# 128 stationary columns for batch 0's value products, and a small rank for the second dispatch in the planned order

## The chip, the core and the metric

The kernel runs on one core of a Trainium2 chip. The metric is device time in microseconds (us) of one execution, from three executions of the kernel, of which the median counts. Beside them stands one profiled execution, whose trace is read below. The engines are PE (TensorE matmul), PEld (TensorE weight load), DVE (VectorE), ACT (ScalarE), POOL (GpSimd) and SP (the engine that issues most of the DMA transfers here).

## What is computed

Four batches of 576 tokens pass through block-causal attention with 8 heads of 64, then a token-mixing layer with two matrices of 512x1024 and 1024x512 and a gate, and then a mixture of eight experts in which each token goes to one expert, all in float32.

```python
scores = scale * np.matmul(q, k.transpose(0, 1, 3, 2))      # 4 batches, 8 heads, 576 x 64
scores = np.where(block_i >= block_j, scores, -1e9)         # blocks of 64
attn = np.exp(scores - max); attn = attn / (attn.sum() + 1e-9)
x = np.matmul(attn, v)                                      # heads side by side: 4 x 576 x 512
...
xk = mu_k * x + (1.0 - mu_k) * x_prev
xr = mu_r * x + (1.0 - mu_r) * x_prev
k = np.maximum(xk @ w_k, 0.0)
x = 1.0 / (1.0 + np.exp(-(xr @ w_r))) * (k * k @ w_v)
...
# one expert e per token, fresh or that of the token before, by a local gate
h = np.maximum(x[b, s] @ w1[e], 0.0)                        # w1: 512 x 1024
out[b, s] = p[e] * (h @ w2[e])                              # w2: 1024 x 512
```

## The kernel before

**The order.** Almost nothing is issued where it is written. Each operation is recorded in a plan, with its engine, an estimated duration and what it depends on, and at the end a list scheduler (`schedule`, L95) simulates the engines and decides the order in which each engine gets its instructions. `Plan.issue` (L273) then emits them, so that nearly every instruction of the trace bears line L282. The hardware doesn't reorder: each engine runs its list in order and waits where an operand isn't ready. Among the operations that are ready on an engine, the scheduler takes the one with the smallest `prio`, which is a due time worked back from the end of the program. To that it adds a rank: `prio -= 1e5 * o[5]` (L109) lowers the number by 100,000 ns of due time where o[5] is true. Before the change o[5] is a yes or no: no for operations recorded under the ranks "ffn" (the expert slots) and "late" (the second dispatch), yes for all else. Where nothing is ready for PE in the first stage, the scheduler puts in a small filler matmul (L1418, `acc<-ones`, bf16).

**Attention.** A unit is one half (256 query rows) of one head of one batch; a half also has its own short list of key chunks. A unit forms scores `s` on PE, maxima `nm` on DVE, exponentials `ea` or `eb` on ACT, transposes them on PE (`psT<-ident,ea` and `psT<-ident,eb`), copies the transposed tiles on ACT to SBUF, and multiplies them with the values (`values`, L651); ACT copies the result to `x`. In batches 1 to 3 scores and values go in two parts each as fp32r, a high and a low one. Batch 0 is `direct` (L513): its matmuls take plain fp32 operands. Its buffers are lent from later stages (`lend`, L403): `v` is one of two tiles of five chunks of 128 keys by 64 columns (tile v itself and the start of tile x_1), the transposed tiles lie in `d`, `xm` and `x_1`. So a value product of batch 0 shows as `acc<-x,v`, `acc<-d,x`, `av<-d,v` and the like, and its form 128*64 is 128 contraction rows by 64 stationary columns; score products and most of the transposes have the form 128*128, and 32 of the transposes (of the first, half-wide key chunk) 128*64. While batch 0 runs, the mixing weights `wk`, `wr`, `wv` are loaded in pieces and split in two by ACT and POOL, after DVE has unpacked them.

**Mixing.** Groups of 256 tokens follow, woven with the attention of batches 1 to 3. Group 0 forms `d` (the difference of neighbouring tokens, POOL), `xm` (DVE), `xh` (ACT) and then multiplies. Its `d` lies in the tile lent to batch 0.

**Experts.** Routing gives each token an expert and a rank. A first dispatch sorts the tokens known by then, and a second one (`dispatch(False)`, L1028, rank "late") sorts the rest: some 60 small DVE operations and a few matmuls that end in `evi` (the expert of each slot, and whether it is another than before), and `gidx` and `sidx` (the token rows that a slot gathers and scatters). Then 19 slots of 128 tokens run (`slot`, L1324). The first seven need only the first dispatch. A slot has POOL gather its rows (`ea<-y_dram,gidx`, L1266), SP read the expert's number from `evi` into a register (L1287 and L1288), SP issue four loads of 512 KB for w1 and four for w2 (L1295) into the only raw buffers that there are (w1: `eb` twice, `qk`, `x`; w2: `x` three times, `d`). Of each such chunk ACT writes the high part and DVE the low part (a 128x1024 subtraction, `wkl<-x,wkh`, `attr<-eb,attr`, `wvl<-eb,wvh`, `xl<-d,kkl`): I call these the wide splits. A raw buffer is free for the next slot's load once DVE has made the low part. The split weights of even and odd slots lie in two sets of tiles (even: w1 in attr, w2 in wkh and wkl; odd: w1 in wvh and wvl, w2 in kkh, xh, kkl, xl). PE transposes the rows, ACT and DVE split them (`wrl<-psT,wrh`, 128x512), PE multiplies with w1, ACT applies relu, PE transposes again and multiplies with w2, ACT scales the result into `xm`, and POOL scatters it (`out<-xm,sidx`, L1275).

Of the kernel before, what the change touches and what calls it, by code (L numbers as in the profile page):

```python
# [9 lines left out]
F32 = mybir.dt.float32  # L10
# [10 lines left out]
B, H, S, D = 4, 8, 576, 64  # L21
# [163 lines left out]
class Plan:  # L185
# [87 lines left out]
    def issue(self):  # L273
        ops = self.ops
        until = next(i for i, o in enumerate(ops) if o[0] == "pe" and o[3][0].tensor.name == self.bank)
        start, order = schedule([(o[0], o[5], o[6], o[8], o[9], o[7][0] not in ("ffn", "late")) for o in ops], until if self.warm else -1, 54.0)
        for i in order:
            if i < 0:
                self.warm()
                continue  # L280
            o = ops[i]
            o[2](*o[3], **o[4])  # L282
# [3 lines left out]
def fused_kernel(ctx: ExitStack, tc: tile.TileContext, a, out):  # L286
# [3 lines left out]
    pe, act, dve, pool, sp = (Engine(plan, n, e) for n, e in zip(  # L290
        ("pe", "act", "dve", "pool", "sp"), (nc.tensor, nc.scalar, nc.vector, nc.gpsimd, nc.sync)))
# [73 lines left out]
    a1 = att.enter_context(tc.tile_pool(name="a1", bufs=1))  # L365
# [3 lines left out]
    def buffers(where, name, shape=None, dtype=F32, n=1):  # L369
        if name not in rings:  # L370
            rings[name] = [0] + [where.tile(shape, dtype, name=f"{name}_{i}") for i in range(n)]
        return rings[name]

    def ring(*args):

        r = buffers(*args)
        r[0] += 1
        return r[1 + (r[0] - 1) % (len(r) - 1)]

    def flat(x):  # L380
        return x.rearrange("p a b -> p (a b)")
# [19 lines left out]
    lent = {}  # L401

    def lend():  # L403
        x0, x1 = (flat(buffers(m1, f"x{i}", [128, 4, (321, 257)[i]], F32, 2)[2]) for i in range(2))
        th = buffers(m1, "th", [128, DM], F32, 2)[1:]
        relu = buffers(m1, "relu", [128, 512], F32, 2)[1:]
        d = flat(buffers(m1, "d", [128, 4, GT])[1])
        xm = flat(buffers(m1, "xm", [128, 2, GT])[1])
        raw = buffers(a1, "wraw", [128, 512], F32, 2)[1:]
        lent["qk"] = [buffers(a1, "qk", [128, NQ + S], F32, 1)[1], x0[:, 0:NQ + S]]  # L410
        lent["v"] = [flat(buffers(a1, "v", [128, 5, D], F32, 1)[1]), x1[:, 0:320]]
        lent["pt00"], lent["pt01"], lent["pt12"] = [d[:, 0:256]], [d[:, 256:640]], [d[:, 640:1024]]
        lent["pt10"], lent["pt11"] = [xm[:, 0:256]], [x1[:, 320:832]]

        for n in ("qk", "pt00", "pt10"):
            for x in lent[n]:
                dve.memset(x[64:128, :], 0.0)
        lent["w"] = [*relu, *th, *raw]
        lent["wt"] = [xm[:, 256:512]]
        lent["avt"] = [x[:, n:n + 256] for n in (0, 256) for x in raw]  # L420

    def borrow(name):
        if not lent:
            lend()
        lent[name].append(lent[name].pop(0))
        return lent[name][-1]
# [82 lines left out]
    class Unit:  # L509
# [35 lines left out]
        def load_v(self):  # L545
            if self.other:
                self.v = self.other.v
                return
            if self.direct:
                self.v = borrow("v").rearrange("p (c d) -> p c d", d=D)  # L550
            else:
                self.v = ring(a1, "v", [128, 5, D], F32, 1)
            sp.dma_start(self.v[:, 0:self.nv, :], a["v"][self.b, self.h][:, 0:self.nv, :])

        def prep_v(self):
# [95 lines left out]
        def values(self):  # L651
            if self.direct and self.half:
                self.av = av = buffers(psA, "acc", [128, 512], F32, 2)[2]
            else:
                self.av = av = ring(psA, "av", [128, 512], F32, 1)
            for c, (t, o, q) in self.at.items():
                hi, lo = (x[:, o:o + 256 - q] for x in self.pt[t])
                last = c == max(self.at)
                if self.direct:
                    pe.matmul(av[0:64, q:256], self.v[:, c, :], hi, start=(c == 0), stop=last)  # L660
                    continue
                if not last:
                    pe.matmul(av[:, q:256], self.vs[:, c, :], hi, start=(c == 0), stop=False)
                if c:
                    pe.matmul(av[0:64, q:256], self.vs[:, c, 0:D], lo, start=False, stop=False)
                if last:
                    pe.matmul(av[:, q:256], self.vs[:, c, :], hi, start=False, stop=True)
# [21 lines left out]
    class First(Unit):  # L689
# [5 lines left out]
        def load(self):  # L695
            self.q0 = 0
            if not lent:
                lend()
            qk = ring(a1, "qk", [128, NQ + S], F32, 1)
            self.q, self.k = qk[:, 0:NQ], qk[:, NQ:NQ + 512]  # L700
            r = 64 if self.b == 0 else 128
            sp.dma_start(qk[0:r, 0:NQ + 512], a["qk0"][self.b, 0:r])
# [579 lines left out]
    def expert(j, always):  # L1282

        e, i = (evi[0], j) if j < EARLY else (evi[1], j - EARLY)

        def issue():
            regs[j] = (nc.sync.value_load(e[0:1, 0, i:i + 1], min_val=0, max_val=NE - 1),  # L1287
                       None if always else nc.sync.value_load(e[0:1, 1, i:i + 1], min_val=0, max_val=1))  # L1288

        return plan.add("sp", "expert", issue, ins=[e], hold=0.0, late=1250.0)  # L1290

    def load(j, raw, src, at):
        def issue():
            e, new = regs[j]
            nc.sync.dma_start(raw, src(e), **({} if new is None else {"cond": new}))  # L1295

        plan.add("sp", "load", issue, outs=[raw], after=[at], hold=800.0 if j >= SLOTS else 400.0)
# [54 lines left out]
    def tiles(ns, count, out, ins, stationary, moving):  # L1352


        def issue():
            for i in ns:
                for t in range(4):
                    nc.tensor.matmul(out[t * ROWS:t * ROWS + ROWS, :], stationary(i, t), moving(i, t),
                                     start=(i == 0), stop=(i == count - 1))

        plan.add("pe", "tiles", issue, outs=[out], ins=ins + [out] * (ns[0] > 0), hold=1000.0)
# [117 lines left out]
```

## Time and profile before

| quantity | value |
|---|---|
| three executions, median | 798.25 us (796.76 to 800.64) |
| profiled execution | 800.11 us, of which its span 798.4 us |
| PE busy | 770.8 us (97% of the span), 5051 instructions |
| PEld busy | 635.1 us (80%) |
| DVE busy | 605.5 us (76%) |
| ACT busy | 535.6 us (67%) |
| POOL busy | 290.9 us (36%) |

A timeline row gives the start and duration of an instruction, the engine, the line, the operation, its result and operands (buffer numbers left out), shapes, and in brackets how long the engine had been idle before it and what ended that. A row of the windows gives, for a stretch of the span, the busy time of each engine, then the granted clock of TensorE (1.00 is full speed), the share of the DMA engines that were busy, and the rate moved. Busy PE is not PE at its peak: the ends of matmuls are modelled, and a matmul that follows another closely overlaps it in the records.

### The profile page before, as it was taken

How to read it: one execution, taken by the hardware profiler on the slowest of the kernel's cores; microseconds unless marked ns; L12 is line 12 of the kernel's file. 1: busy time of each engine (PE TensorE's matmuls, PEld its weight loads, DVE VectorE, ACT ScalarE, POOL GpSimd, SP SyncE). 2: the span in 40 equal slices, each digit the busy share in tenths (PEclk: the TensorE clock that was granted, in tenths of full speed). 3: DMA queues.
4: the chain of work that ended last, by engine and by line, in shares of the span. 5: the costliest groups of instructions: out<-in, count | busy, mean ns of one | idle time of the engine just before them, and what ended most of it. 6: DMA issues, size and time to landing. Idle time of an engine off the chain costs nothing.

```text
span 798.4 us, 14950 instructions
## 1 busy us (share of the span) xinstructions
PE 770.8 (97%) x5051; PEld 635.1 (80%) x5051; DVE 605.5 (76%) x1301; ACT 535.6 (67%) x1156; POOL 290.9 (36%) x275
## 2 busy tenths in 40 slices
PE   8999999999999999999999998999998999999993
PEld 8665798988989989898997977778876767677872
DVE  6987757876678769587786489899998978588820
ACT  3888567893578946266893525688848968678830
POOL 3334585543745537264452324121121202122100
PEclk9999999999999999999999999999999999999997
DMA  8566311221223202201310005201546377782032
GB/s 218 156 184 192 108 57 55 90 72 36 78 65 101 95 22 83 70 36 37 100 46 27 2 26 194 85 27 41 171 159 247 118 275 250 240 304 97 31 132 64
DMA packets 40466, 87.62 MB, mean 110 GB/s; under 512 B 6540, under 2 KB 10640, under 8 KB 40384
## 3 DMA queue, kind: packets, MB, share of 16 engines
q1 hardware_dynamic: 37152, 76.71, 29.6%
q0 software_dynamic: 3232, 9.90, 3.4%
q8 instruction: 41, 0.67, 0.4%
q14 instruction: 41, 0.34, 0.1%
HBM read 131.68 MB, written 9.90 MB: 177 GB/s over the span
## 4 chain that ended last, share of the span: by engine, by line
PE 67%; issue 12%; DVE 7%; DMA 6%; ACT 5%; POOL 2%; SPq 0%; POOLq 0%; ACTq 0%
PE acc L282 37%; PE s L282 13%; PE psT L282 8%; PE av L282 6%; PE acc L1418 2%; ACT attr L282 2%; DMA out<-xm,sidx 2%; DMA out<-v,ssum 1%; DMA ea<-y_dram,gidx 1%; DVE xm L282 1%; DMA qk<-in_w 1%; ACT ea L282 1%; DMA wraw<-in_w 1%; DVE attr L282 1%; DMA th<-in_w 1%
## 5 line engine op out<-in xcount | busy, mean ns | idle before, releaser
L1275 POOL DMA_INDIRECT out<-xm,sidx x19 | 22.1, 1162 | 174.9 <-ACT xm L282 172.3
L282 DVE TENSOR_REDUCE nm<-s 128x1 f32<-128x576 f32 (+4 forms) x132 | 67.7, 547 | 21.2 <-ACT s L282 20.2
L282 PE MATMUL acc<-xh,wkh 128*128 128x256 f32 x288 | 81.4, 292 | 0.3 <-DVE rk L282 0.3
L282 PE MATMUL acc<-xl,wkh 128*128 128x256 f32 x288 | 81.1, 289 | 0.7 <-POOL xl L282 0.6
L282 PE MATMUL acc<-xh,wkl 128*128 128x256 f32 x288 | 80.5, 288 | 0.0
L282 POOL TENSOR_TENSOR attr<-qk,attr 64x512 fp32r<-64x512 f32 (+1 forms) x48 | 66.9, 1393 | 37.1 <-ACT attr L282 32.4
L282 PE MATMUL av<-attr 128*128 128x256 f32 (+3 forms) x336 | 78.2, 287 | 0.1
L282 DVE TENSOR_TENSOR attr<-psT,attr 64x256 fp32r<-64x256 f32 (+2 forms) x120 | 63.0, 525 | 15.9 <-ACT attr L282 13.6
L282 POOL TENSOR_TENSOR kkl<-relu,kkh 128x512 fp32r<-128x512 f32 x36 | 46.6, 1297 | 56.8 <-ACT kkh L282 47.3
L282 PE MATMUL s<-attr 128*128 128x288 f32 (+3 forms) x288 | 67.1, 299 | 0.0
L282 POOL TENSOR_TENSOR xl<-xm,xh 128x512 fp32r<-128x512 f32 x36 | 46.4, 1288 | 51.9 <-ACT xh L282 46.9
L282 PE MATMUL acc<-attr,wrh 128*128 128x512 f32 x160 | 60.2, 409 | 0.0
L282 ACT ACTIVATE attr<-psT 64x256 fp32r<-64x256 f32 (+2 forms) x120 | 53.4, 462 | 9.2 <-PE psT L282 6.9
L282 PE MATMUL acc<-wvh,kkh 128*128 128x512 f32 x144 | 56.4, 416 | 1.9 <-ACT th L282 1.9
L282 DVE TENSOR_TENSOR wrl<-psT,wrh 128x512 fp32r<-128x512 f32 x57 | 39.2, 687 | 24.2 <-ACT wrh L282 23.8
L282 ACT ACTIVATE xh<-xm 128x512 fp32r<-128x512 f32 x36 | 22.7, 631 | 49.9 <-DVE xm L282 48.8
L282 PE MATMUL acc<-wvh,kkl 128*128 128x512 f32 x144 | 55.6, 413 | 0.0
L282 PE MATMUL acc<-wvl,kkh 128*128 128x512 f32 x144 | 55.2, 408 | 0.0
L282 PEld LDWEIGHTS av<-attr 128*128 128x128 f32 (+1 forms) x336 | 51.5, 166 | 4.7 <-issue 0.6
L282 PEld LDWEIGHTS acc<-xh,wkh 128*128 128x128 f32 x288 | 53.3, 189 | 2.2 <-ACT s L282 0.5
L282 PEld LDWEIGHTS acc<-xl,wkh 128*128 128x128 f32 x288 | 53.4, 189 | 1.9 <-POOL xl L282 1.1
L282 PE MATMUL psT<-ident,eb 128*128 128x128 f32 (+1 forms) x288 | 54.2, 277 | 0.0
(355 smaller groups left out, 2393.1 us busy)
## 6 DMA issues: line engine op xcount, KB each, us to landing
x<-in_w SPq DMA_DIRECT2D x76, 512.0 KB
eb<-in_w SPq DMA_DIRECT2D x38, 512.0 KB
qk<-in_qk SPq DMA_DIRECT2D x24, 544.0 KB
qk<-in_w SPq DMA_DIRECT2D x19, 512.0 KB
d<-in_w SPq DMA_DIRECT2D x19, 512.0 KB
wraw<-in_w SPq DMA_DIRECT2D x24, 256.0 KB
y_dram<-th SPq DMA_DIRECT2D x18, 256.0 KB
v<-in_v SPq DMA_DIRECT2D x28, 160.0 KB
```

The lines of the kernel that those rows point to most:

```text
L282: o[2](*o[3], **o[4])
L1275: plan.add("pool", "scatter", lambda: nc.gpsimd.indirect_dma_start(out=out, out_offset=bass.IndirectOffsetOnAxis(ap=at.bitcast(U32), axis= ...
L1418: plan.warm = lambda: pe.matmul(first[:, 0:128], ones, ones, start=True, stop=True)
```

## The change

In batch 0 a value product takes two neighbouring chunks of `v` as its stationary operand, 128 columns instead of 64. The first 64 columns give the wanted result in rows 0 to 63, and the other 64 give rows 64 to 127, which nobody reads. So that the last chunk has a neighbour, the tiles grow from five to six chunks, the sixth being zeros from two new memsets, and one lent tile moves by 64 columns. The second part replaces the yes or no of the rank by a number: 0 for "ffn", 0.2 for "late", 1 for all else. At L109 that is 20,000 ns of due time by which the second dispatch goes ahead of the expert slots' operations. The changed file is four lines longer from `lend` on, so that L1287 is there L1291, and L1295 is L1299.

```diff
-        start, order = schedule([(o[0], o[5], o[6], o[8], o[9], o[7][0] not in ("ffn", "late")) for o in ops], until if self.warm else -1, 54.0)
+        start, order = schedule([(o[0], o[5], o[6], o[8], o[9], {"ffn": 0.0, "late": 0.2}.get(o[7][0], 1.0)) for o in ops], until if self.warm else -1, 54.0)
...
-        lent["v"] = [flat(buffers(a1, "v", [128, 5, D], F32, 1)[1]), x1[:, 0:320]]
+        lent["v"] = [flat(buffers(a1, "v", [128, 6, D], F32, 1)[1]), x1[:, 0:384]]
+
+        for x in lent["v"]:
+            dve.memset(x[:, 320:384], 0.0)
...
-        lent["pt10"], lent["pt11"] = [xm[:, 0:256]], [x1[:, 320:832]]
+        lent["pt10"], lent["pt11"] = [xm[:, 0:256]], [x1[:, 384:896]]
...
-                self.v = ring(a1, "v", [128, 5, D], F32, 1)
+                self.v = ring(a1, "v", [128, 6, D], F32, 1)[:, 0:5, :]
...
-                    pe.matmul(av[0:64, q:256], self.v[:, c, :], hi, start=(c == 0), stop=last)
+                    pe.matmul(av[:, q:256], self.v[:, c:c + 2, :].rearrange("p c d -> p (c d)"), hi,
+                              start=(c == 0), stop=last)
```

The order on PE hardly changes in batch 0, but the form does. About in the middle of the batch there stands in PE's row before (the last numbers are the stationary columns by the moving ones):

```order
L282 MATMUL psT_140<-ident,eb_147 128x128 x3
L282 MATMUL acc_152<-xm_129,v_133 64x256
L282 MATMUL av_141<-d_128,v_133 64x256 x2
L282 MATMUL s_0_134<-qk_132 128x192
L282 MATMUL acc_152<-x_1_123,v_133 64x256
L282 MATMUL psT_139<-ident,ea_136 64x128
```

and in the changed kernel:

```order
L282 MATMUL psT_140<-ident,eb_147 128x128 x3
L282 MATMUL acc_152<-xm_129,v_133 128x256
L282 MATMUL av_141<-d_128,v_133 128x256 x2
L282 MATMUL acc_152<-x_1_123,v_133 128x256
L282 MATMUL psT_139<-ident,ea_136 64x128
L282 MATMUL s_0_134<-qk_132 128x192
```

The value products have 128 columns now, the one transpose has 64 as before, and a score product moved behind them.

On DVE the second dispatch ends in `gidx_110`. Before, its end stands among the splits of slot 6's w2 (`wkl`):

```order
L282 TENSOR_TENSOR evi_107<-es 1x18
L282 CAST evi_107<-es 1x18
L282 TENSOR_TENSOR wkl<-x_0_122,wkh 128x1024
L282 TENSOR_TENSOR wkl<-x_1_121,wkh 128x1024
L282 COPY d_inv_191<-s_0_134 128x110
L282 TENSOR_TENSOR wrl<-psT_140,wrh 128x512
L282 TENSOR_TENSOR d_inv_191<-d_inv_191 128x22
L282 TENSOR_TENSOR wkl<-x_1_123,wkh 128x1024
L282 TENSOR_SCALAR gidx_110<-d_inv_191 128x18
L282 TENSOR_TENSOR wkl<-d_128,wkh 128x1024
```

In the changed kernel it stands at the start of the splits of slot 4's w2 (`wkl`) and of slot 5's w1 (`wvl`):

```order
L282 COPY d_inv_191<-s_0_134 128x110
L282 TENSOR_TENSOR evi_107<-es 1x18
L282 CAST evi_107<-es 1x18
L282 TENSOR_TENSOR d_inv_191<-d_inv_191 128x22
L282 TENSOR_TENSOR wkl<-x_0_122,wkh 128x1024
L282 TENSOR_SCALAR gidx_110<-d_inv_191 128x18
L282 TENSOR_TENSOR wvl<-eb_147,wvh 128x1024
```

Eighteen wide splits and six of the 128x512 splits, which stood ahead of `gidx_110`, stand behind it now; ahead of `evi_107<-es` there are 16 and 5 fewer. The first operation of this dispatch after the routing, `d_sob`, moved by 11 wide splits.

On SP the reading of `evi_107` (slot 7's expert) stands before behind the last loads of slot 6's w2 (`x_1_123`, `d_128`), and slot 7's first load follows it:

```order
L1295 DMA x_1_123<-in_w 128x2x512
L1295 ISA
L1295 DMA d_128<-in_w 128x2x512
L1287 TENSOR_LOAD evi_107
L1287 ISA x2
```

and in the changed kernel between the last load of slot 5's w2 (`d_128`) and the first load of slot 6's (`x_0_122`):

```order
L1299 DMA d_128<-in_w 128x2x512
L1291 TENSOR_LOAD evi_107
L1291 ISA x2
L1292 TENSOR_LOAD evi_107
L1292 ISA x2
L1299 ISA
L1299 DMA x_0_122<-in_w 128x2x512
```

Slot 7's loads can stand among those of slot 6's w2 there, while before all of slot 6's loads had to be issued first.

## Rows read from the trace of the kernel before

**Rows 1.** Windows of batch 0: busy time of each engine, granted clock, DMA, GB/s

```profile
20.00:40.00 20.00, 20.00 (x106) 13.09 (x103) 18.48 (x43) 16.91 (x58) 7.58 (x10) 1.00 0.53 156
40.00:60.00 20.00, 19.93 (x104) 12.13 (x104) 16.32 (x44) 16.21 (x53) 7.98 (x11) 1.00 0.63 184
60.00:80.00 20.00, 20.00 (x101) 11.49 (x102) 14.86 (x37) 16.90 (x57) 9.28 (x12) 1.00 0.61 190
80.00:92.00 12.00, 12.00 (x107) 8.34 (x106) 8.87 (x24) 8.63 (x21) 6.15 (x8) 1.00 0.37 105
```

**Rows 2.** Chain of waits, 20 to 92 us: its shares, then start, us, link

```profile
by line: PE s L282 28.8%; PE acc L282 26.8%; PE psT L282 24.2%; PE av L282 12.4%; PE acc L1418 4.9%; ACT ea L282 1.4%; ACT x L282 0.7%; ACT wrh L282 0.5%; issue 0.3%; ACT s L282 0.1%; ACTq L282 0.0%
...
23.54 0.57 PE av L282 x2
...
49.71 0.76 PE s L282 x4
...
53.42 0.58 PE acc L282 x2
53.99 0.43 PE av L282 x2
...
54.98 0.33 PE psT L282 x3
...
59.99 0.48 PE psT L282 x3
...
89.15 0.79 PE acc L282 x4
```

**Rows 3.** Timeline of PE, one row of the same stretch

```profile
54.82 0.49 PE L282 MATMUL psT<-ident,ea 128*128 128x128 f32 x3
```

**Rows 4.** Weight loads grouped by form, 20 to 92 us: busy, mean ns, idle

```profile
L282 PEld LDWEIGHTS s<-x 128*128 128x128 f32 x48 | 7.9, 193 | 1.7 <-issue 1.1 <-ACT wkh L282 0.4
...
L282 PEld LDWEIGHTS av<-d,v 128*64 128x64 f32 x24 | 2.9, 136 | 2.0 <-issue 0.7 <-ACT eb L282 0.2
```

**Rows 5.** Timeline of POOL at the end of batch 0

```profile
90.03 1.89 POOL L282 TENSOR_TENSOR d<-x 128x1024 f32<-128x1024 f32 x1 [0.35 <-PE acc L282]
```

**Rows 6.** Windows of the second dispatch

```profile
560.00:580.00 20.00, 20.00 (x99) 16.06 (x98) 19.34 (x54) 16.79 (x22) 2.89 (x3) 1.00 0.53 170
...
600.00:610.00 10.00, 6.76 (x26) 5.19 (x27) 7.21 (x7) 7.64 (x11) 2.63 (x2) 0.83 1.03 395
```

**Rows 7.** Timeline of DVE around the second dispatch

```profile
545.66 0.17 DVE L282 CAST d_sob<-so 128x8 bf16<-128x8 f32 x1
...
552.96 1.22 DVE L282 TENSOR_TENSOR xl<-d,kkl 128x1024 fp32r<-128x1024 f32 x1
...
594.75 0.16 DVE L282 TENSOR_SCALAR gidx<-d_inv 128x18 int32<-128x18 f32 x1
```

**Rows 8.** DVE groups by form, 545.6 to 594.8 us: busy, mean ns, idle

```profile
L282 DVE TENSOR_TENSOR wrl<-psT,wrh 128x512 fp32r<-128x512 f32 x12 | 8.2, 686 | 1.3 <-ACT wrh L282 1.3
L282 DVE TENSOR_TENSOR wkl<-x,wkh 128x1024 fp32r<-128x1024 f32 x6 | 7.2, 1210 | 0.0
```

**Rows 9.** Timeline of POOL: the scatters of slots 3 to 6

```profile
572.44 1.02 POOL L1275 DMA_INDIRECT out<-xm,sidx  x1 [9.51 <-ACT xm L282]
...
585.55 1.49 POOL L1275 DMA_INDIRECT out<-xm,sidx  x1 [12.09 <-ACT xm L282]
...
603.00 1.69 POOL L1275 DMA_INDIRECT out<-xm,sidx  x1 [4.42 <-ACT xm L282]
...
616.90 1.03 POOL L1275 DMA_INDIRECT out<-xm,sidx  x1 [10.70 <-ACT xm L282]
```

**Rows 10.** Timeline of SP, ACT and PE, the stretch of Rows 7

```profile
593.54 0.99 SPq L1295 DMA_DIRECT2D eb<-in_w  x2
...
602.06 0.67 ACT L282 ACTIVATE xm<-s,pslot 128x512 f32<-128x512 f32 x1
...
568.23 0.39 PE L282 MATMUL s<-xl,wrh 128*128 128x512 f32 x1
...
602.78 0.50 PE L282 MATMUL s<-wkh,wrh 128*128 128x512 f32 x1 [2.85 <-ACT xm L282]
```

## The prediction

> **What bounds the kernel now.** The two parts of the change act in two stages, so each is read from its own. The first view is the windows of batch 0 [rows 1]: PE is busy 19.93 to 20.00 of every 20 us at full granted clock from 20 to 92 us, while DVE sums to 58.5 and ACT to 58.6 of the 72 us. The chain of waits of that stretch [rows 2] says the same by another road: its shares of PE are 28.8 + 26.8 + 24.2 + 12.4 + 4.9, 97% in all. The reader is to see that in batch 0 hardly a wait of PE for anyone counts, so that what PE does not have to do is time, up to the point at which DVE or ACT ends last.
>
> The same chain shows that this busy PE loses time. It gives each link the time that PE really moved on. A pair of 256-column value products that follows another pair took 0.43 us (the second link at 53.99), a pair that follows something else 0.58 (at 53.42): entering a run of value products costs 0.15 us. Three transposes took 0.33 us behind a score product (54.98) and 0.48 behind value products (59.99): leaving a run costs 0.15 as well. The score products cost no such thing: four in 0.76 us (at 49.71) [rows 2], 0.19 each for 224 columns, is 0.85 ns a column, and the pair at 53.99 has 0.43 / 512 = 0.84. What the value products have and the scores have not is the form 128*64, the fp32 matmul with 64 stationary columns [rows 4].
>
> The third view is the second dispatch, where the end of the kernel is decided by the slots' scatters [rows 9]. They follow each other in 13.11 us (572.44 to 585.55), then 17.45 (to 603.00) and 13.90 (to 616.90). Two regular spacings would be 26.2 us; 31.35 were taken, so 5.1 us are lost at slot 5 and 6. The rows of the other engines say why [rows 10]: SP issued slot 7's first weight load at 593.54 only, ACT took that slot's high parts in the order written for it, with slot 5's result `xm` (602.06) queued behind them, and PE waited 2.85 us for `xm` (602.78). From 600 to 610 us PE was busy 6.76 of 10 us at a granted clock of 0.83 in the mean [rows 6]: some of that time TensorE ran at 1.2 GHz instead of 2.4, after the wait. SP couldn't issue earlier since slot 7's expert comes out of the second dispatch, whose DVE part ran from 545.66 to 594.75 [rows 7] between the wide splits.
>
> **Part one, the value products.** It adds no matmul and no column that streams: the stationary operand grows, the moving one doesn't. It removes the entry and the exit of each run of value products. I counted 38 runs in batch 0, the first and last of them at 23.54 and 89.15 [rows 2]. 38 x (0.15 + 0.15) = 11.4 us of PE time: by window 9 runs and 2.7 us from 20 to 40, 11 and 3.3 from 40 to 60, 18 and 5.4 from 60 to 92. What it could cost is the longer weight load: 193 ns against 136 in the mean [rows 4], 57 ns more, and 128 such loads' matmuls make 7.3 us if each were exposed and nothing if hidden. I take nothing, because the score products have loads of 128 columns, and by the 0.85 ns a column above they lose no time to them. So PE's own saving lies between 4.1 and 11.4, and I take 11.4.
>
> How much of it becomes time depends on who is late next. DVE has idle time of 1.5, 3.7, 5.1 and 3.1 us in the four windows and ACT 3.1, 3.8, 3.1 and 3.4 [rows 1]. The first window can give at most 1.5, the second 3.3 (PE's own), the last two together 5.4 (PE's own, against 6.5 and 8.2 idle): 10.2 us is the cap. The other end is the one window where both engines have more idle time than PE saves, 3.3 us. After a saving of 10 DVE and ACT would be busy 58.5 of 62 us, and every unit passes from PE to DVE and ACT and back, so some of the room will be waits. I take the middle, 7 us, and keep 3.3 and 10.2 for the range. The time carries on: group 0's `d` on POOL starts 0.35 us after the last value product at 90.03 [rows 5] and the mixing hangs on it.
>
> The rest of part one is small. Two memsets of 128x64 on DVE at the start are of the size of the smallest instructions there, 0.17 us each by `d_sob` [rows 7], and the start of the program waits for loads; 0 to 0.3 us, and I take 0. The lent tile that moves keeps its size and its users.
>
> **Part two, the second dispatch.** Nothing is added; it moves. 18 wide splits and 6 of the 128x512 ones now stand behind `gidx`. A wide split takes 1210 ns alone and a 128x512 split 686 [rows 8], some 0.08 less when they follow closely: 18 x 1.13 + 6 x 0.6 = 24 us by which `gidx` comes earlier, at 571 instead of 594.75. By 16 and 5 of them `evi` comes 21 us earlier. SP then has slot 7's expert long before a raw buffer is free, and its loads start when DVE has freed the buffers of slot 6's w1 instead of at 593.54. The 5.1 us lost at slots 5 and 6 should go: 0 if something else holds slot 7 as late, 5.1 if nothing does.
>
> What is pushed back pays. Of the 49.1 us of the dispatch [rows 7] some 25 wide and 12 short splits take 25 x 1.13 + 12 x 0.6 = 35.5, so 13.6 us are dispatch proper. Splits that stood ahead of it are late by up to that. The split `xl<-d,kkl` (slot 3's last chunk of w2) ended at 554.18 [rows 7] and PE first used it at 568.23 [rows 10]: 14 us of cover, just enough. DVE is busy 19.34 of 20 us there [rows 6], so it catches up only as the dispatch ends, and each raw buffer is freed as much later, with SP's next load queued on it. I take 1.6 us of new waits on PE between 545 and 580, with 0 and 5 as the ends. SP's new wait for `evi`, at about 569, has slot 6's w2 loads queued behind it; these can't start before slot 5's w2 is split, which stands later in DVE's row, so I cost it at nothing; if that cover were gone it is the load of one chunk late. Part two: 5.1 - 1.6 = 3.5 us, between 0 and 5.1 (the lower end below nothing is the last rival).
>
> **The sum.** 7 + 3.5 = 10.5 us. The profiled execution took 800.11 us (1.7 of them outside its span), so it would be 789.6; it lies 1.9 above the median of 798.25, within the runs shown, so the same difference goes to the median: 798.25 - 10.5 = 787.75, put as 787.8.
>
> **Rules beside the rows.** Three transposes stand in one row [rows 3], which carries the form of the first; the second of them has 64 stationary columns. Their link took 0.33 us (at 54.98) [rows 2], the plain 0.11 each, so a transpose of 64 among others of 128 costs nothing there. The Trainium skill, in "TensorEngine Tiling (Array Packing)", Tiling Modes, Key Properties, says that a change of the tiling mode, not of the tile alone, drains TensorE. By that, the losses at the value products' entries and exits would be drains, as the rows agree, but the transposes with 64 columns, which remain, would drain too; there the rows do not agree. "TensorE: Matmul & The Clock Gate", Part 3, The mechanism, of the Trainium skill says that a weight load overlaps running matmuls only where its row group differs. By that the longer loads of full height would be exposed; the score products above speak against it.
>
> **The rivals.** (A) All of PE's saving and all of part two arrive: 10.2 + 5.1 = 15.3, so 783.0. For it: 97% of the chain on PE. Against it: DVE's 18.48 of 20 in the first window. (B) DVE and ACT take PE's place in batch 0: 3.3 + 3.5 = 6.8, so 791.4. For it: 58.5 busy of some 62; against it: the idle time of both is spread, and they have room now. (C) The loss moves to the transposes: with the scores and values at 128 columns the 32 transposes of 64 pay 0.30 us each, 9.6 of the 11.4; 1.8 + 3.5 = 5.3, so 793.0. This is what the drain rule would do; the row at 54.82 speaks against it. (D) The longer loads are exposed: 4.1 + 3.5 = 7.6, so 790.7. (E) The change doesn't do what it says, since the entries and exits come from the alternation of buffers and not from the 64 columns: nothing in batch 0, and 798.25 - 3.5 = 794.8. (F) Slower: the dispatch put first on a DVE with no room starves slots 3, 4 and 5 of their splits, each of which then costs what slot 5 and 6 lose now, 5.1 us: 15.3 lost against 5.1 won and 7 in batch 0, so 801.5, and 805 with 3.3 in batch 0. It decides once PE's waits for splits between 545 and 590 us pass 12.1 us. For it: 19.34 of 20 busy and 14 us of cover against 13.6 of delay. Against it: most splits are late by less, as the dispatch is still spread among 14 or more of them.
>
> **How the numbers follow.** The forecast has 0.48, A 0.16, B 0.13, C 0.04, D 0.04, E 0.08, F 0.07. About 0.5%, 4.0 us, is what a measurement of this kernel can tell from no change; that puts the bounds at 794.3 and 802.2. Below 794.3 lie the forecast, A, B, C and D, 0.85, where what strays out of them makes up for the part of E that comes in with 5.1 from part two. Within lie the rest of E and the nearer half of F, 0.11; above 802.2 the farther half of F, 0.04. The range runs from 781.5 (A with all 11.4 us of PE's saving instead of 10.2 gives 781.75) to 793.5 (just beyond C), and leaves out E and F, 0.15, and a little of A.
>
> **What the profile after would show.** In the chain of batch 0, pairs of 256-column value products at 0.43 us wherever they stand, and three transposes in 0.33 us behind them; the last value product some 7 us before 90.03. If it is B, PE's busy time in the windows falls below 19, with waits for DVE and ACT; if C or D, PE stays at 20 of 20 and the entries or single records stay long. In the second stage, `gidx` about 24 us earlier relative to slot 3's scatter, slot 7's first load not behind slot 6's last, scatters of slots 5 and 6 some 13 us apart, and no stretch with a granted clock of 0.83 there. I am wrong on the whole if PE's waits for splits from 545 to 590 us sum to more than 5, or if batch 0 ends less than 3 us earlier.

## The result, and the profile after

| | before | changed kernel |
|---|---|---|
| median | 798.51 us (796.76 to 802.08) | 791.70 us (787.76 to 794.12) |
| ratio, 95% interval | | 0.990 (0.9874 to 0.9926) |
| profiled execution, of which span | 800.11, 798.4 us | 787.76, 786.0 us |

The change makes the kernel faster by about 8 us by the ratio, 6.8 by the medians. The forecast was 10.5 us, with a range that holds the measured time. The profiled execution of the changed kernel is the fastest of its six, and the one before lay above its median, so the spans differ by 12.4 us where the medians differ by 6.8. A second execution was therefore profiled (e3 below, 791.8 us), and a reading counts here where both traces have it.

The windows of batch 0 in the changed kernel, with columns as in [rows 1]:

```profile
20.00:40.00 20.00, 19.71 (x117) 16.64 (x115) 19.18 (x46) 18.04 (x62) 9.00 (x12) 1.00 0.61 178
40.00:60.00 20.00, 19.00 (x110) 15.60 (x110) 19.26 (x46) 17.66 (x60) 8.80 (x12) 1.00 0.72 206
60.00:80.00 20.00, 19.59 (x131) 15.73 (x130) 19.38 (x45) 18.01 (x57) 9.51 (x14) 1.00 0.53 167
```

PE, first, is no longer busy all of the time (19.00 to 19.71 of 20 us), and DVE, third, is about as full as PE, at 19.18 to 19.38 (18.33 to 19.26 in the second trace) where it had 14.86 to 18.48. Pieces of the chain of waits in the changed kernel (start, us, link), which answer to [rows 2]:

```profile
57.29 1.45 PE s L282 x6
58.74 0.43 PE acc L282 x2
59.17 0.11 PE psT L282
59.28 0.35 PE s L282 x2
59.63 0.33 PE psT L282 x3
59.96 0.43 PE acc L282 x2
```

A pair of value products behind a score product (58.74) or behind transposes (59.96) takes 0.43 us, as only a later pair did before, and the transpose behind it (59.17) takes 0.11: both the entry and the exit are gone. (The six score products of the first piece are four of 224 columns and two of 288.) The end of batch 0, on POOL, answers to [rows 5]:

```profile
82.66 1.90 POOL L282 TENSOR_TENSOR d<-x 128x1024 f32<-128x1024 f32 x1 [0.56 <-PE acc L282]
```

It came 7.37 us earlier. The scatters of slots 3 to 6 answer to [rows 9]:

```profile
564.76 1.87 POOL L1279 DMA_INDIRECT out<-xm,sidx  x1 [9.84 <-DMA x<-in_w]
...
582.74 2.08 POOL L1279 DMA_INDIRECT out<-xm,sidx  x1 [14.78 <-ACT xm L282]
...
597.02 1.02 POOL L1279 DMA_INDIRECT out<-xm,sidx  x1 [10.30 <-DVE wvl L282]
609.25 1.57 POOL L1279 DMA_INDIRECT out<-xm,sidx  x1 [9.03 <-ACT xm L282]
```

The spacings were 13.1, 17.5 and 13.9 us. Now they are 18.0, 14.3 and 12.2: the wait didn't go, it moved one slot forward. Rows of the changed kernel's timeline around it, of DVE, SP, ACT and PE, which answer to [rows 7, 10]:

```profile
560.43 0.16 DVE L282 TENSOR_SCALAR gidx<-d_inv 128x18 int32<-128x18 f32 x1
...
565.13 0.34 SPq L1299 DMA_DIRECT2D eb<-in_w  x1
567.65 0.34 SPq L1299 DMA_DIRECT2D qk<-in_w  x1
...
572.93 1.06 ACT L282 ACTIVATE attr<-qk 128x1024 fp32r<-128x1024 f32 x1 [2.68 <-DMA qk<-in_w]
573.89 0.58 ACT L282 ACTIVATE wrh<-psT 128x512 fp32r<-128x512 f32 x1
...
574.52 0.50 PE L282 MATMUL s<-wkh,wrh 128*128 128x512 f32 x1 [2.18 <-ACT wrh L282]
```

The window of the changed kernel in which the wait lies, with columns as in [rows 6]:

```profile
570.00:580.00 10.00, 7.82 (x29) 5.76 (x28) 7.23 (x7) 5.23 (x7) 0.00 (x0) 0.83 0.91 324
```

`gidx` stands 4.3 us ahead of slot 3's scatter; before, it stood 22.3 behind it [rows 7, 9]. So the second dispatch is 26.6 us earlier on DVE relative to the slots. But ACT now waits 2.68 us for the third chunk of slot 6's w1 (`qk`), slot 4's `wrh` is queued behind that, PE waits 2.18 us for `wrh`, and the mean granted clock of these 10 us falls to the 0.83 that stood at 600 to 610 us before [rows 6]. The second trace has the same 0.83 from 572 to 582 us. PE's waits from 525 to 620 us in the changed kernel (engine, result, line, what it waited for: us in total, times, longest):

```profile
PE s L282 <- ACT wrh L282: 2.2, 1, 2.2
PE psT L282 <- ACT relu L282: 1.8, 1, 1.8
PE acc L282 <- ACT wrh L282: 0.6, 1, 0.6
PE s L282 <- DVE wrl L282: 0.5, 1, 0.5
```

The first and the third are the waits between 545 and 590 us, 2.8 us in all, and 4.0 in the second trace.

### The profile page after: what moved, and what is told of

It is laid out like the page before. It is cut to its first block, busy times and chain, and to the rows that moved or that the text cites. A ratio compares the mean times of both kernels' runs of the same rounds, so it can differ in the third digit from the quotient of the medians.

```text
span 786.0 us, 14915 instructions
## 1 busy us (share of the span) xinstructions
PE 758.1 (96%) x5036; PEld 639.2 (81%) x5036; DVE 608.6 (77%) x1303; ACT 534.7 (68%) x1156; POOL 299.8 (38%) x275
## 4 chain that ended last, share of the span: by engine, by line
PE 57%; issue 13%; DMA 11%; DVE 10%; ACT 7%; POOL 1%; SPq 1%; POOLq 0%; DVEq 0%; ACTq 0%
PE acc L282 34%; PE s L282 10%; PE psT L282 7%; PE av L282 5%; DMA out<-xm,sidx 3%; DMA d<-in_w 2%; DVE xm L282 2%; DMA th<-in_w 2%; DMA out<-v,ssum 1%; ACT attr L282 1%; DVE nm L282 1%; ACT ea L282 1%; DVE attr L282 1%; PE acc L1422 1%; DVE wraw L282 1%
## 5 line engine op out<-in xcount | busy, mean ns | idle before, releaser
L1279 POOL DMA_INDIRECT out<-xm,sidx x19 | 27.9, 1471 | 164.8 <-ACT xm L282 137.1
```

The lines of the kernel that those rows point to most:

```text
L1279: plan.add("pool", "scatter", lambda: nc.gpsimd.indirect_dma_start(out=out, out_offset=bass.IndirectOffsetOnAxis(ap=at.bitcast(U32), axis= ...
```

## The experiments

### The two parts apart

e1, part one alone (of a changed line, only the term that changes is shown, here and in e2 and e7):

```diff
-{"ffn": 0.0, "late": 0.2}.get(o[7][0], 1.0)
+o[7][0] not in ("ffn", "late")
```

> Part one alone: the value products of batch 0 with 128 stationary columns, the second dispatch without a rank of its own, as before. Theory: batch 0 carries all of the gain and the second dispatch none. Group 0's d on POOL starts near 82.7 us as in the changed kernel (90.03 before), slots 4 to 6 are scattered with the spacings of before (one of about 17.5 us, then about 14), and the time is 7 to 9 us below the kernel before, 789.5 to 791.5, as fast as the changed kernel or faster. Rival, the terms of the prediction: part two carries 3.5 us, so this kernel is 7 us below before and 3 to 4 us slower than the changed one.

Measured: 791.98 us, ratio 0.9907 (0.988 to 0.9934). `d` started at 83.07 us; the spacings at slots 4 to 6 were 13.0, 18.1 and 13.1.

e2, part two alone:

```diff
-o[7][0] not in ("ffn", "late")
+{"ffn": 0.0, "late": 0.2}.get(o[7][0], 1.0)
```

> Part two alone: the second dispatch with rank 0.2, the value products with 64 columns as before. Theory: the wait at slot 5 goes, but a new one at slot 4 takes its place (SP reads slot 7's expert and issues more loads into a fuller DMA, ACT waits for slot 6's w1 with slot 4's products queued behind), so the time is within 1.5 us of the kernel before, 797 to 800; in the trace a spacing of some 18 us at slot 4 instead of 17.5 at slot 5. Rival, the term of the prediction: 3.5 us faster than before, 795, with spacings of 13 at slots 4 to 6.

Measured: 800.74 us, ratio 1.0015 (0.9997 to 1.0034); `d` at 89.96, spacings 17.4, 16.0 and 12.2. The two longest of PE's waits from 500 to 620 us there, in the same columns as above:

```profile
PE s L282 <- ACT wrh L282: 3.6, 2, 2.9
PE psT L282 <- ACT th L282: 2.1, 2, 1.6
```

Part one carries all of the result, and part two nothing that can be told from zero. The term of 3.5 us falls.

e3, the changed kernel once more:

> The changed kernel once more, for a second trace and more times. Theory: the wait at slot 4 lies in the order and not in one execution, so the second trace has a spacing of 17 to 19 us there again; the times are 788 to 794 with a median near 791.5. Rival: the wait is an accident of the one execution, the second trace has spacings of 12.5 to 14 at slots 3 to 6, and what differs between executions (787.8 to 794.1) is this wait.

Measured: 792.50 us (790.79 to 795.53), ratio 0.9916 (0.989 to 0.9943), `d` at 83.03, spacing 19.2 us at slot 4, ACT's wait for `qk` 3.6 us. The wait lies in the order; the rival is out.

### What ends batch 0 now

e4 leaves out an operation of the unpacking, and the scheduler plans without it:

```diff
-                    dve.scalar_tensor_tensor(top, low, 29, top, op0=ALU.logical_shift_right, op1=ALU.bitwise_or)
```

> The changed kernel, without the last of the three DVE operations that unpack each half chunk of the mixing weights (the three lowest bits of their mantissas are left out): 48 operations of some 0.5 us less on DVE, nearly all of them in batch 0. Theory: after the change DVE (with ACT fed by it) ends last in batch 0, so with DVE relieved by some 20 us PE is the bound again and group 0's d on POOL starts 3 to 4 us earlier than in the changed kernel, at 78.5 to 80 us instead of 82.66, the whole 3 to 4 us faster than the changed kernel. Rival: the passing from engine to engine or ACT alone sets the end of batch 0, d starts at 82 to 83 and the time stays.

Measured: 793.76 us, ratio 0.991 (0.9872 to 0.9948), `d` at 85.22, later than in the changed kernel, though DVE was busy only 10.78 of the 20 us from 60 to 80. This decides nothing: the scheduler, given other durations, had made another order, and two things were changed at once.

e5 mends that. The plan records the operation in full, and what is issued works on 8 columns, so the order is exactly that of the changed kernel:

```diff
-                    dve.scalar_tensor_tensor(top, low, 29, top, op0=ALU.logical_shift_right, op1=ALU.bitwise_or)
+                    plan.add("dve", "scalar_tensor_tensor", part, (top, low, 29, top),
+                             dict(op0=ALU.logical_shift_right, op1=ALU.bitwise_or))
...
+    def part(o, x, n, y, **kw):
+        nc.vector.scalar_tensor_tensor(o[:, 0:8], x[:, 0:8], n, y[:, 0:8], **kw)
```

> The changed kernel in exactly its own order, but the third of the three DVE operations that unpack each half chunk of the mixing weights works on 8 of its 256 columns (the lowest bits of the rest are left out): some 48 operations of about 0.1 us in place of about 0.5, 18 us less on DVE in batch 0. Theory: DVE ends last in batch 0 after the change, so group 0's d on POOL starts 3 to 4 us earlier, at 78.5 to 80 us in place of 82.66 and 83.03 in the two traces, and the whole is 2 to 4 us faster than the changed kernel. Rival: ACT (18.0 of 20 us busy in a window) or the passing between engines sets the end of batch 0: d starts at 82 to 83.

Measured: 790.75 us, ratio 0.9879 (0.9846 to 0.9912), `d` at 81.00. The window from 20 to 79 us of e5, with columns as in [rows 1]:

```profile
20.00:79.00 59.00, 58.09 (x356) 48.45 (x355) 48.48 (x137) 54.00 (x179) 26.46 (x36) 1.00 0.63 190
```

The same window of the changed kernel:

```profile
20.00:79.00 59.00, 57.30 (x345) 47.07 (x343) 56.82 (x132) 53.45 (x177) 26.64 (x35) 1.00 0.63 187
```

DVE had 8.3 us less to do in this stretch, not the 18 that I expected (32 narrowed operations of 0.19 us fell into it, where I had counted 48 of 0.1, and 5 more of DVE's instructions), and batch 0 ended 1.7 us earlier than in the first trace of the changed kernel, 2.0 than in the second: half of what the theory asked for. So DVE is a part of what ends batch 0 now; relieved of it, ACT has 54.0 of 59 and PE 58.1. The time of the whole, 790.75 us, can't be told from that of the changed kernel. The shares of the chain of waits in the changed kernel from 20 to 92 us answer to [rows 2] (the last 9 us lie behind batch 0, and the view breaks off at its right edge):

```profile
by line: issue 12.1%; PE s L282 9.9%; PE acc L282 9.3%; PE acc L1422 8.3%; DVE nm L282 7.2%; DVE xm L282 7.2%; PE psT L282 6.8%; ACT eb L282 5.5%; ACT ea L282 5.2%; DVE relu L282 4.6%; DVE wraw L282 4.2%; ACT d L282 3.2%; ACT wvh L282 2.5%;
```

PE has about a third of it, where it had 97%, and DVE and ACT most of the rest. In the second trace, from 20 to 84 us, PE has a fifth, and POOL's splits of the mixing weights stand in the chain. So no single engine ends batch 0 now.

e12, part one for the second halves only, without part two:

```diff
+                if self.direct and not self.half:
+                    pe.matmul(av[0:64, q:256], self.v[:, c, :], hi, start=(c == 0), stop=last)
+                    continue
                 if self.direct:
```

> Part one for the second halves of batch 0's heads alone (those with the longer list of keys): their value products have 128 stationary columns, the first halves' 64 as before; the second dispatch as before. In PE's row 17 runs of products with 64 columns are left of 38, so by 0.30 us each PE saves 6.3 us instead of 11.4. Theory: PE's saving becomes time one for one until DVE and ACT end last, so group 0's d on POOL starts 5.5 to 6.3 us before 90.03, at 83.7 to 84.5, not far from the 82.5 to 83.5 of the full change; in what is left of the 64-column runs the first pair still takes 0.58 us. Rival: each run removed is worth the same, about two thirds of its price, all the way: 90.03 less 7.1 x 21 / 38 = 3.9 us, d at 86.1.

Measured: 793.02 us, ratio 0.9943 (0.9926 to 0.9959). The start of `d` in its timeline:

```profile
84.78 1.90 POOL L282 TENSOR_TENSOR d<-x 128x1024 f32<-128x1024 f32 x1 [0.21 <-ACT wvh L282]
```

Two links of its chain of waits, start, us and link:

```profile
49.44 0.43 PE acc L282 x2
49.88 0.58 PE av L282 x2
```

The shares of the chain in e12 from 20 to 84 us:

```profile
by line: PE s L282 32.6%; PE psT L282 21.5%; PE acc L282 20.3%; PE av L282 17.4%; ACT ea L282 1.6%; POOL attr L282 1.6%; DVE xm L282 1.3%; ACT wkh L282 1.0%; issue 1.0%; PE acc L1425 0.9%; DVE attr L282 0.6%; DVE ea L282 0.6%; DVE th L282 0
```

Two pairs, one behind the other: the one with 128 columns takes 0.43 us, the one with 64 behind it 0.58. The loss sits where runs of 64-column products begin and end. 21 runs fewer gave 5.25 us, 0.25 each of a price of 0.30, with over 90% of the chain still on PE. The other 17 gave 84.78 less 82.8 (the mean of the nine traces that have all of part one, 82.52 to 83.46), 2.0 us or 0.12 each. That is the bend that the theory expects: PE's saving is nearly all time, until the other engines end last.

### What makes the wait at slot 4

The trace offers two causes for the late `qk`. SP reads the experts of later slots between slot 6's loads; its records of such readings follow each other by 0.58 us (566.47, 567.05, 567.63 and 568.21 in e6), there are two for a slot, and in the changed kernel three of them stand between the issues of `eb` at 565.13 and of `qk` at 567.65. And the first small slot's four loads are issued right behind `qk`. e6 takes the small slots' loads out of the way, e6b the readings as well, and e9 the readings alone.

The first two changes are in all three, the third (small slots) in e6 and e6b, the last (slots) in e6b and e9.

```diff
-        plan.add("sp", "load", issue, outs=[raw], after=[at], hold=800.0 if j >= SLOTS else 400.0)
+        last[j] = plan.add("sp", "load", issue, outs=[raw], after=[at], hold=800.0 if j >= SLOTS else 400.0)
...
-        return plan.add("sp", "expert", issue, ins=[e], hold=0.0, late=1250.0)
+        return plan.add("sp", "expert", issue, ins=[e], hold=0.0, late=1250.0, after=after)
...
-        at = expert(j, True)
+        at = expert(j, True, [last[BEFORE[q] - 2]])
...
-        at = expert(j, always)
+        at = expert(j, always, [last[j - 2]] if EARLY <= j < MAIN else [])
```

> The changed kernel, with the loads of each small slot put behind the last load of the slot two before the one it precedes (slot 7 for the first small slot). Theory: at slot 4 ACT waits for the third chunk of slot 6's w1 (qk) because SP issues it late, behind the reading of later slots' experts (some 2.2 us), and because the four loads of the first small slot, issued right behind it, share the DMA; without the latter the spacing at slot 4 falls from 18.0 and 19.2 us to 16 to 17.5, and the time by 1 to 2 us against the changed kernel. Rival: the loads of the small slot don't matter, spacing 18 to 19 and no difference in time.

Measured: 792.25 us, ratio 0.9905 (0.9878 to 0.9931), spacing at slot 4 19.1. Nothing gained, but a fourth reading came to stand between `eb` and `qk` there, so that `qk` was issued 3.5 us behind slot 3's scatter (569.19) instead of 2.9. From its issue to ACT's start on it 5.3 us passed without the small loads behind it, where the two traces of the changed kernel have 5.3 and 6.5 with them.

> As the run before, and each slot from the eighth on has its expert read only behind the last load of the slot two before it, so that no reading stands between the loads of slot 6. Theory: both causes are gone, qk of slot 6 is issued some 2 us earlier and lands by 570, the spacing at slot 4 falls to 13 to 15 us, and the time is 3 to 5 us below the changed kernel, 787 to 789. Rival: the weights of slots 6 and 7 and the DMA's rate set it whatever the order of SP: spacing 17 or more, or the same wait one slot later, and less than 1 us of difference.

Measured: 788.43 us, ratio 0.9847 (0.9819 to 0.9875), spacings 13.9, 15.8 and 12.4; the first of them and the time are as the theory had them. `qk` was issued 1.1 us behind slot 3's scatter (567.49), 1.8 earlier than in the changed kernel, which is three readings of 0.58. ACT's row for `qk` in the timeline of e6:

```profile
574.50 1.06 ACT L282 ACTIVATE attr<-qk 128x1024 fp32r<-128x1024 f32 x1 [3.00 <-DMA qk<-in_w]
```

and in that of e6b:

```profile
571.65 1.06 ACT L282 ACTIVATE attr<-qk 128x1024 fp32r<-128x1024 f32 x1 [0.37 <-DMA qk<-in_w]
```

> The changed kernel with only the readings moved: each slot from the eighth on has its expert read behind the last load of the slot two before it; the loads of the small slots stand where the scheduler puts them, here among those of slot 6. With the three runs before it makes a square: neither moved 791.7 to 792.5, small loads moved 792.25, both moved 788.4. Theory: the readings are the main cause of the wait at slot 4 and the small slots' loads a lesser one that shows only without them; spacing at slot 4 of 14 to 16 us, time 789 to 791. Rival: it takes both, since the loads among slot 6's now delay qk by as much as the readings did: spacing 17 to 19, 791.5 to 793.

Measured: 790.85 us, ratio 0.9892 (0.9864 to 0.992), spacing 17.1: the spacing of the rival, a time at the upper end of the theory's, and no gain over the changed kernel that its interval can tell. Without the readings, three of the small slot's loads come up ahead of slot 6's first chunk, and it is this chunk that ACT waits for, and no longer `qk`:

```profile
571.38 1.06 ACT L282 ACTIVATE attr<-eb 128x1024 fp32r<-128x1024 f32 x1 [3.89 <-DMA eb<-in_w]
```

So it takes both: the readings moved, and the small loads kept from taking their place.

### How far ahead

e7 gives rank 1, as below, e10 rank 0 and e11 rank 0.1; e7 starts from the changed kernel, e10 and e11 from e6b.

```diff
-{"ffn": 0.0, "late": 0.2}.get(o[7][0], 1.0)
+{"ffn": 0.0, "late": 1.0}.get(o[7][0], 1.0)
```

> The changed kernel with rank 1 in place of 0.2 for the second dispatch, as all work ahead of the slots has it: its last DVE operation stands some 28 rows earlier still, the experts of slots 7 and on are read earlier, and the loads of the first small slot come up before slot 5's. Theory: the earlier dispatch only moves the same wait: time within 3 us of the changed kernel, one spacing of 16 to 19 us at slots 3 to 5. Rival of the change's own idea: the earlier the better, 2 to 4 us faster.

Measured: 796.39 us, ratio 0.9954 (0.9932 to 0.9976), 4 to 5 us slower than the changed kernel. The spacings from slot 2 on are 12.1 to 12.9 us up to slot 7, and the list of PE's waits is empty there, but more than that is paid ahead, where PE has the dispatch's matmuls queued in front of the slots'. In the timeline of PE in e7:

```profile
526.09 0.71 PE L282 MATMUL s<-d_rhs,wraw 128*128 128x110 bf16 x6 [7.07 <-DVE d_rhs L282]
```

PE waits 9.1 us in all for `d_rhs`, and slot 0's scatter comes at 538.82 instead of 524.68. The expectation of another 16 to 19 us at slots 3 to 5, and of a time within 3 us, was wrong; a wait of another kind took its place.

> The kernel with readings and small loads moved (788.4 us), with rank 0 for the second dispatch as before the change. Theory: the earlier dispatch is worth something only once SP's readings are out of the way; at rank 0 the expert of slot 7 comes too late again, with a spacing of some 17 to 18 us at slot 5, so 791 to 793, 3 to 4 us slower than with rank 0.2. Rival: the moved readings carry the whole 3.5 us, and the rank nothing: 788 to 789.

Measured: 788.86 us, ratio 0.9878 (0.985 to 0.9905), spacings 13.1, 16.9 and 15.2. By the time the rival holds: with no rank at all, moving SP's readings and the small loads is worth 2 to 3 us over e1, though the intervals of the two overlap. It isn't the wait at the slots that went. From slot 0's scatter to slot 6's e10 took 84.2 us and e1 83.1; the gain stands behind slot 6, 168.7 us to the last scatter against 172.4, and its cause is open. In e6b the first stretch is 82.0 and the second 170.6. So with SP's queue cleared the earlier dispatch does shorten its own stretch, by 2.1 us in these two traces, and nearly as much is lost behind it.

> The kernel with readings and small loads moved, with rank 0.1 in place of 0.2: the last operation of the second dispatch stands 11 rows later on DVE. Theory: with the dispatch less far ahead the splits of slots 3 to 5 are less late and the expert of slot 7 still comes before its buffers are free, so the spacings at slots 4 and 5 (13.9 and 15.8 us with 0.2) fall to 13 to 15 and the time to 787 to 788. Rival: the loads of slots 6 and 7 in the DMA set them and not the rank, so 788 to 789.5.

Measured: 790.86 us, ratio 0.9909 (0.9877 to 0.9942), spacings 15.6, 17.7 and 12.4. Neither theory nor rival: slower than rank 0.2, and than rank 0 by the medians alone, since those intervals overlap. I have no cause for it beyond the spacings. Of the kernels run, e6b at 788.43 us has the lowest median, 3 us below the changed kernel; its lead over e10 is not settled, since their intervals overlap.

## Why the prediction was right, and where its sum was wrong

**The bound and the price of a run: right.** That PE alone set batch 0 and that each run of 64-column value products cost 0.15 us at either end shows in the chain after: 0.43 for a pair that stands behind a score product or transposes, 0.11 for the transpose behind it. e12 has both cases side by side.

**The longer weight loads at nothing: right.** The loads of the value products take 190 to 194 ns in the mean in the changed kernel instead of 136, and the pairs still take 0.43. Rival D is out. So is C: the transpose at 59.17 has 64 stationary columns and stands between a value product and a score product of 128, at 0.11 us. The Trainium skill, in "TensorEngine Tiling (Array Packing)", Tiling Modes, Key Properties, states a drain for a change of tiling mode. The losses at the 64-column value products would fit one and the 64-column transposes show none; no run here shows which of them is such a change.

**7 us of it become time: right in size, in part by luck.** Nine traces have `d` at 82.8 us in the mean, 7.2 earlier. That the other engines would cut off a part of PE's 11.4 us was foreseen, and 4.2 us were cut off; e5 and the chain show that DVE, ACT and PE share the end. But 7 was the middle between two bounds, and the lower one doesn't follow from its rows: 3.3 was to be the one window in which both engines have more idle time than PE saves, while from 60 to 92 us the prediction itself has 6.5 and 8.2 us idle against a saving of 5.4.

**Part two, 5.1 us recovered less 1.6 us of new waits: wrong.** This is the step that failed; it was worth -3.5 us and measured +1.2 (-0.2 to +2.7) alone. The first half of its mechanism came true: `gidx` came 26.6 us earlier where 24 were forecast, and slot 7's loads no longer stood behind all of slot 6's. But between the scatters of slots 0 and 6 the kernel before took 83.3 us and e1 83.1, the changed kernel 84.6 and 85.8, and e2 85.6: 1.3 to 2.7 us more, not 3.5 less. The new waits of PE, put at 1.6 us, were 2.8 and 4.0 from 545 to 590 us, less than the 5 that I had named as the sign of being wrong, and with them went a stretch at a granted clock of 0.83 that the price didn't have. They were as large as those removed, and they came not from late splits on DVE, as I had priced them, but from SP, whose late `qk` held ACT and so `wrh`. I had counted its new wait for `evi` and costed it at nothing, and not the time that the readings themselves take, which now stand between the loads that PE needs next. The prediction had looked at SP's order, which shows the readings, but put a price only on DVE. The wait before had them in it already: `evi` was ready at 590.55 us, when SP had just been let go by slot 6's last load (590.52), and of the 3.0 us from there to slot 7's first load four readings took 2.3 (590.95 to 593.27). So that load did not wait for the dispatch alone, as the prediction says. Rival F had the sign of this part, but by another mechanism, and far too large.

A part of this came back later. From slot 6's scatter to the last, the kernel before took 173.1 us and e1 172.4, but the changed kernel 168.4 and 169.5, and e2 171.4. In the waits from 620 us on, PE waited 3.6 us for the small slots' weights before and 0.8 in the changed kernel, where the first of their loads are issued earlier (568.65 instead of 601.20); no run tests this by itself. For e2, where PE waited 3.0 us, that isn't the cause, and it stays open what shortened those slots there.

**The sum.** Of the 10.5 us forecast, 6.8 came, and what is missing is about what part two was given. The measured 791.7 us lies next to rival B's 791.4, but only by number: B has 3.3 us from batch 0 and 3.5 from part two, and the runs show 7.2 and nothing that can be told from zero.

## What to carry to other kernels

Where an engine is the bound, compare what the same instruction costs behind its like and behind another kind; a loss that has no row of its own, such as the 0.15 us at each change of form, shows only so, and wider operands that do useless work can remove it. Such a gain is nearly all time until the next engines are full (0.25 us of a price of 0.30 here, then 0.12), so read their room window by window before claiming it. When an order is moved forward, price every instruction that moves with it on every queue, register readings between loads included: freeing one wait early can be worth nothing if it puts readings in front of the next load.

## What was unexpected of the hardware

A register reading on SP took 0.58 us from one to the next, nearly what a load of 512 KB takes from its issue to the next (0.64 us, from 593.54 to 594.18 before), and 28 such readings stand between 500 and 790 us. A fp32 matmul pair of 256 columns takes the same 0.43 us with 64 and with 128 stationary columns, so the other half of the columns is to be had for no time; it is the neighbourhood of the two forms that costs, and only where the 64 columns are a value product's, not a transpose's.
